# A four-layer sequence model on one core: identity multiplications at the start, diagonals and factors on VectorE, an order table per task

## The chip, the core and the metric

One core of one Trainium2 chip. The metric is the device time of the whole kernel in microseconds; the runs of one kernel in this study spread over 0.2 to 1.3%. Engines in the profile: PE is TensorE, PEld its weight loads, DVE is VectorE, ACT ScalarE, POOL GpSimd, SP the engine that issues most DMAs.

## The reference

Four layers on a sequence of 2048 tokens with 640 features, in bf16: A, B, A, B, each on the normalized input and with a residual.

```python
def _A_ref(x, ...):                      # state space layer ("S5")
    Lam_bar = jnp.exp(dt * Lam)                               # 640 complex numbers
    B_bar = ((Lam_bar - 1.0) / Lam)[:, None] * Bmat           # the "factors" scale B (or C)
    Bu = jnp.einsum("bld,pd->blp", x + 0j, B_bar)
    for t in range(L):
        h = Lam_bar[None, :] * h + Bu[:, t, :]
        ...
    return 2.0 * jnp.einsum("blp,dp->bld", hseq, Cmat).real + x * Dskip[None, None, :]

def _B_ref(q, k, v, ...):                # q, k, v are inputs: the long convolution does not depend on x
    ...                                  # k_shift: shift convolution of k with 4 taps
    kv = k_shift * v
    ...                                  # y: convolution of kv with ssm_k over 2048 steps, by FFT
    y = y + kv * ssm_D[None, None, :]
    return q * y

x = x + _A_ref(_layernorm(x), ...);  x = x + _B_ref(_layernorm(x), ...)
x = x + _A_ref(_layernorm(x), ...);  x = x + _B_ref(_layernorm(x), ...)
```

## The kernel before

The program is a set of tasks with an engine, an estimated duration, dependencies and buffer slots. While it is built, a list scheduler in Python plays them through and so fixes the order of the instructions on each engine; all PSUM is four slots of 128 x 1024 fp32. A table gives each group of tasks a number that makes up most of its rank.

```python
    WHEN = {"yt_io0": -1077.9, ..., "a_lamd": 156.7, "a_f": 165.3, ...}     # subtracted: makes up most of the rank
    ...
    cands = [t for t in ready if eng in t.engs and (t.engs[0] == eng or eng_free[t.engs[0]] > now + 0.3) and can(t)]
    t = max(cands, key=lambda t: (t.rank, -t.idx))
```

The diagonals and factors are made on GpSimd:

```python
    def diag(dst, scal, n):
        nc.gpsimd.tensor_tensor(dst, ident[:, None, :].to_broadcast([P, n, P]), scal[:, :, None].to_broadcast([P, n, P]), ALU.mult)

    def e_lamd(_):                                            # 15 diagonals of 128: "wide diagonals"
        diag(s_ld.get().rearrange("p i j n -> p (i j) n"), st["lam"][:].rearrange("p i j -> p (i j)"), 15)
    t_ld = S.add("a_lamd", "pool", 3.4, [t_lam], e_lamd, uses=[s_ld])

    def e_f(_):                                               # the factors, on 128 x 5 elements
        v = nc.gpsimd
        v.tensor_tensor(den[:], lre, lre, ALU.mult)
        ...                                                   # some 25 more such instructions
    t_f = S.add("a_f", "pool", 5.5, [t_lam], e_f)
    ...
        def e_dk(_, kb=kb, s_ds=s_ds):                        # diagonals of the shift convolution, 512 wide
            nc.gpsimd.tensor_tensor(s_ds.get(), consts["ident_bf"][:, None, :].to_broadcast([P, 4, P]),
                                    st["skf"][:, :, kb:kb + 1].to_broadcast([P, 4, P]), ALU.mult)
```

TensorE multiplies them: the shift convolution is 8 matmuls of 512 columns per half, B times the wide diagonals gives the matrices of the second token phase. A PSUM slot is free for the next group only when ScalarE or VectorE has evicted it. In a B layer each of four rows has its own product and sum on VectorE:

```python
                def e_m(_, q=q, bu=bu):
                    b, x = bu(), s_x.get()[:, q, :]
                    nc.vector.tensor_tensor(b, b, s_Y.get()[:, q, :], ALU.mult)
                    ...                                       # sum with x, by layer
```

Of the kernel before, what the change touches and what calls it, by code (L numbers as in the profile page):

```python
# [17 lines left out]
P = 128  # L18
# [34 lines left out]
    "yt_io0": -1077.9, "yt_ph0": -1019.3, "yt_sin0": 190.5, "yt_neg0": 314.5, "yt_io6": -1435.7, "yt_ph6": -1019.8, "yt_sin6": -1080.4, "yt_neg6": 172.3,  # L53
    "yt_io12": 294.3, "yt_ph12": -1069.6, "yt_sin12": 375.6, "yt_neg12": 156.6, "yt_Ci": 118.7, "yt_Si": 403.1, "yt_nsi": 236.7, "yt_f0": -965, "yt_f2":
    -1540, "yt_f3": -1887, "yt_f4": 179, "yt_h0": 174.5, "yt_h1": 154.3, "yt_h2": 148.5, "yt_h3": 189.9, "kv_dsl": 34.9, "kv_kd": 410.2, "kv_k0": -1067.5,
    "kv_k1": 205.4, "kv_k2": 230.3, "kv_d0": -1030.9, "kv_d1": -1037.8, "kv_d2": 125.1, "kv_ds0": 95.3, "kv_lk0": -919.4, "kv_lv0": 119.4, "kv_mm0":
    -1408, "kv_ev0": 192.8, "kv_st0": -966.5, "kv_ds1": 400.8, "kv_lk1": 143.9, "kv_lv1": 406.3, "kv_mm1": 238.5, "kv_ev1": 232.1, "kv_st1": 180.1,
    "kv_ds2": -1696.5, "kv_lk2": 390.3, "kv_lv2": 173.4, "kv_mm2": 244.3, "kv_ev2": 403.7, "kv_st2": -1020, "kv_ds3": -1063.8, "kv_lk3": -1121.4,
    "kv_lv3": 669.8, "kv_mm3": 420.7, "kv_ev3": -1025, "kv_st3": 1400.2, "kv_ds4": 90.8, "kv_lk4": -926.2, "kv_lv4": 7.3, "kv_mm4": 33, "kv_ev4": -831.9,
    "kv_st4": -980.1, "a_pl": 481.2, "a_p0": -840.7, "a_p1": -1244.2, "a_p2": 1659, "a_p3": 156.5, "a_p4": -793.6, "a_p5": 225.8, "a_p6": -1643.5,  # L60
    "a_lamd": 156.7, "a_f": 165.3, "a_dd": 521.1, "a_ldB0": 150.8, "a_ldB1": -1247.6, "a_wl00": -1403.1, "a_wc00": -1264.8, "a_wm00": 209.8, "a_wl01":
    75.8, "a_wc01": -881, "a_wm01": 418.7, "a_wl02": 307.9, "a_wc02": 301.4, "a_wm02": 403.5, "a_wl03": 164, "a_wc03": -903.2, "a_wm03": -1083.3,
    "a_wl04": 357.2, "a_wc04": -1099.8, "a_wm04": 601.7, "a_b00": 178, "a_b0e0": 230.3, "a_b01": 173.9, "a_b0e1": -1067.1, "a_b10": 69.2, "a_b1e0":
    -1516.7, "a_b11": -1560.6, "a_b1e1": 508.8, "a_gm0": -1359.9, "a_ge0": -1048.3, "a_gm1": -727, "a_ge1": -1525.1, "a_gm2": -1618.5, "a_ge2": -1376.9,
    "a_gm3": -1641.8, "a_ge3": -1386.3, "a_gm4": -1643.2, "a_ge4": -1403, "a_wl10": -2.6, "a_wc10": 155, "a_wm10": -1068.5, "a_wl11": 159.1, "a_wc11":
    -965.4, "a_wm11": 184, "a_wl12": -818.1, "a_wc12": -1242.6, "a_wm12": 79.5, "a_wl13": 104.8, "a_wc13": 414.8, "a_wm13": 181.4, "a_wl14": -1008.6,
    "a_wc14": 26.2, "a_wm14": -1248.1, "a_ti": -1521.4, "a_ta": 395.3, "a_t0": -829.9, "a_t1": 170.8, "a_t2": 613.8, "yq0_kl": -982.4, "yq0_ka": -1602.5,
    "yq0_KA": 159.8, "yq0_KB": 402.8, "yq0_vl": -1113.3, "yq0_VA": 481.3, "yq0_VB": -1118.9, "yq1_kl": 30, "yq1_ka": 311.3, "yq1_KA": -1517.3, "yq1_KB":
    -954.5, "yq0_pw": 209.4, "yq0_IB": 298.2, "yq0_tt": -1552, "yq1_vl": 1519.1, "yq1_VA": -1096.8, "yq1_VB": 420.6, "yq0_IA": 407.6, "yq0_st": -1537.5,
    "yq2_kl": 435.6, "yq2_ka": 157.2, "yq2_KA": 277.9, "yq2_KB": -1166.2, "yq1_pw": 360.8, "yq1_IB": -871.2, "yq1_tt": -1130.5, "yq2_vl": -1467.1,  # L70
    "yq2_VA": 23.2, "yq2_VB": 25.8, "yq1_IA": -1377.8, "yq1_st": -1484.6, "yq3_kl": 498, "yq3_ka": 1686.9, "yq3_KA": 438.7, "yq3_KB": -1402.5, "yq2_pw":
    1355.7, "yq2_IB": -1302.1, "yq2_tt": -1424, "yq3_vl": -834.2, "yq3_VA": 161.1, "yq3_VB": 86.9, "yq2_IA": 2.9, "yq2_st": 300.2, "yq4_kl": -1275,
    "yq4_ka": 618.1, "yq4_KA": -931.8, "yq4_KB": 225.6, "yq3_pw": -1643.5, "yq3_IB": 331.5, "yq3_tt": -814.8, "yq4_vl": -798.8, "yq4_VA": 157.4, "yq4_VB":
    326.4, "yq3_IA": 628.2, "yq3_st": 404.5, "yq4_pw": 594.6, "yq4_IB": 599.4, "yq4_tt": -1071.8, "yq4_IA": 126.1, "yq4_st": -1404, "xl0": -1622.2,
    "A1c0_ln_bn": 302.5, "A1c0_ln_sd": -1096.7, "A1c0_ln_post": -1648.8, "A1c0_id": -1304.5, "A1c0_tu": -1475.7, "A1c0_bp": 10.7, "A1c0_ev": 355.4,
    "A1c0_ri": 62.1, "A1c0_sc": 641.6, "A1c0_cy": 233.1, "A1c0_ro": -1576.9, "A1c0_xr": 396.2, "A1c0_cp": 627.9, "A1c0_xe": -1443.8, "xl1": -978,
    "A1c1_ln_bn": 221, "A1c1_ln_sd": 479.8, "A1c1_ln_post": -942.2, "A1c1_id": 1422.5, "A1c1_tu": -1312.3, "A1c1_bp": 338.4, "A1c1_ev": 192.1, "A1c1_ri":
    1654.8, "A1c1_sc": -1000.3, "A1c1_cy": -1122.1, "A1c1_ro": -1077.3, "A1c1_xr": 627.3, "A1c1_cp": -1539.8, "A1c1_xe": -1077.9, "xl2": -1346.1,
    "A1c2_ln_bn": 611.3, "A1c2_ln_sd": -1123.4, "A1c2_ln_post": 402.2, "A1c2_id": 141, "A1c2_tu": 96.1, "A1c2_bp": 640.8, "A1c2_ev": -867.9, "A1c2_ri":
    22, "A1c2_sc": 40.1, "A1c2_cy": -1431.1, "A1c2_ro": -1012.6, "A1c2_xr": 471.5, "A1c2_cp": -1082.5, "A1c2_xe": -1450.9, "xl3": 672.8, "A1c3_ln_bn":  # L80
    37.8, "A1c3_ln_sd": -1392.7, "A1c3_ln_post": -1339.6, "A1c3_id": 30.4, "A1c3_tu": 252.1, "A1c3_bp": -1329.6, "A1c3_ev": 410.6, "A1c3_ri": -1152.5,
    "A1c3_sc": 383.7, "A1c3_ro": 185.7, "A1c3_xr": 534.8, "A1c3_cp": 257.2, "A1c3_xe": -1166.6, "yl0": 143.2, "B1c0_ln_nm": 627.2, "B1c0_ln_sq": 628.8,
    "B1c0_ln_sd": 604.7, "B1c0_ln_post": 185.1, "B1c0_u": -1662.7, "B1c0_m": 369.5, "A2c0_ln_nm": 202.2, "A2c0_ln_sq": 222, "A2c0_ln_sd": 59.4,
    "A2c0_ln_post": -1459.4, "A2c0_id": 273.5, "A2c0_tu": 215.4, "A2c0_bp": 72.8, "A2c0_ev": -1459.1, "A2c0_ri": -790.3, "A2c0_sc": -1361.1, "A2c0_cy":
    -1371.9, "A2c0_ro": -1371.9, "A2c0_cp": 348.7, "A2c0_xe": 634.5, "yl1": 669.8, "B1c1_ln_nm": 308.3, "B1c1_ln_sq": 369.1, "B1c1_ln_sd": 59.5,
    "B1c1_ln_post": 617.9, "B1c1_u": 409, "B1c1_m": -805.6, "A2c1_ln_nm": -1007.9, "A2c1_ln_sq": 422.1, "A2c1_ln_sd": 197.3, "A2c1_ln_post": 131.4,
    "A2c1_id": 423.7, "A2c1_tu": 550.3, "A2c1_bp": 151.8, "A2c1_ev": 590.1, "A2c1_ri": -1014.6, "A2c1_sc": -1015.2, "A2c1_cy": -1015.5, "A2c1_ro": 641.4,
    "A2c1_cp": 487.2, "A2c1_xe": -1744.8, "yl2": -1648.1, "B1c2_ln_nm": 322.3, "B1c2_ln_sq": -1642.8, "B1c2_ln_sd": -1510.7, "B1c2_ln_post": 363.6,
# [68 lines left out]
class Sched:  # L157
# [3 lines left out]


    DMA = ((1.3, 1.6), (0.8, 1.6))

    base = 0.0

    def __init__(self, tc):
# [1271 lines left out]
```

## Time and profile before

| | kernel before |
|---|---|
| time, median of 4 runs | 360.49 us (360.18 to 360.77) |
| span of the profiled run | 358.5 us |
| matmul work at full clock (from counts and shapes) | 320.6 us |
| first transform group starts | 18.78 us |
| last matmul ends | 347.88 us |

The prediction below shows the main lines. One more view is needed: what TensorE waited for up to 36 us (engine, line, releaser: total us, times, longest).

```profile
PE ps L501 <- POOL b L401: 1.2, 1, 1.2
```

TensorE stood still 1.2 us for GpSimd's wide diagonals (line 401). This is a wait that the change is meant to remove.

**Lateness.** Below I use one number per stage: the start of the stage's first matmul less the work of all matmuls that the program has ahead of it (N / 2.4 + 2.5 ns each, 25 ns at least; multiplications that only keep TensorE busy count as no work). It tells by how much TensorE is late there, whatever caused it. The values before stand in the tables below.

### The profile page before, as it was taken

How to read it: one execution, taken by the hardware profiler on the slowest of the kernel's cores; microseconds unless marked ns; L12 is line 12 of the kernel's file. 1: busy time of each engine (PE TensorE's matmuls, PEld its weight loads, DVE VectorE, ACT ScalarE, POOL GpSimd, SP SyncE). 2: the span in 40 equal slices, each digit the busy share in tenths (PEclk: the TensorE clock that was granted, in tenths of full speed). 3: DMA queues.
4: the chain of work that ended last, by engine and by line, in shares of the span. 5: the costliest groups of instructions: out<-in, count | busy, mean ns of one | idle time of the engine just before them, and what ended most of it. 6: DMA issues, size and time to landing. Idle time of an engine off the chain costs nothing.

```text
span 358.5 us, 8291 instructions
## 1 busy us (share of the span) xinstructions
PE 324.3 (90%) x3467; PEld 242.3 (68%) x3493; DVE 321.8 (90%) x482; ACT 253.2 (71%) x399; POOL 24.4 (7%) x57
## 2 busy tenths in 40 slices
PE   2888899978997989999999999999999999999980
PEld 1357867867685978886776686688655788756550
DVE  8979999777899669989997998999999799999996
ACT  6589976989499999784598199796618681106861
POOL 6447200000000000000000000000000000000000
PEclk9999999999999999999999999999999999999996
DMA  9999999989996970966095722450032043000231
GB/s 202 227 169 190 205 193 196 235 156 201 241 249 125 237 159 2 144 121 206 2 206 140 273 76 48 117 129 2 14 61 76 0 112 112 1 2 0 85 136 73
DMA packets 118711, 45.90 MB, mean 128 GB/s; under 512 B 111629, under 2 KB 112914, under 8 KB 118674
## 3 DMA queue, kind: packets, MB, share of 16 engines
q1 hardware_dynamic: 118528, 45.36, 59.1%
q8 instruction: 27, 0.44, 0.5%
q14 instruction: 10, 0.08, 0.1%
q10 hardware_dynamic: 146, 0.01, 0.0%
HBM read 17.38 MB, written 7.86 MB: 70 GB/s over the span
## 4 chain that ended last, share of the span: by engine, by line
PE 62%; ACT 14%; DVE 11%; DMA 5%; issue 4%; POOL 2%; SPq 1%; ACTq 0%; DVEq 0%; POOLq 0%
PE ps L773 31%; PE ps L687 9%; PE ps L684 9%; ACT b L296 8%; PE ps L522 4%; PE ps L1064 4%; DMA b<-b 2%; DVE b L298 2%; ACT b L466 1%; DMA b<-in_A_C_im_dram 1%; DMA b<-in_A_C_re_dram 1%; SPq L462 1%; PE ps L1214 1%; DVE b L1070 1%; PE ps L1215 1%
## 5 line engine op out<-in xcount | busy, mean ns | idle before, releaser
L296 ACT ACTIVATE b<-ps 128x1024 bf16<-128x1024 f32 (+3 forms) x121 | 105.9, 957 | 28.9 <-PE ps L687 22.2
L773 PEld LDWEIGHTS <-b 128*128 128x128 bf16 x880 | 67.6, 98 | 48.2
L773 PE MATMUL ps<-W,b 128*128 128x512 bf16 (+1 forms) x632 | 95.4, 299 | 0.4
L684 PE MATMUL ps<-b,BT 128*128 128x256 bf16 x400 | 56.7, 273 | 2.4 <-ACT b L296 1.7
L687 PE MATMUL ps<-b,BT 128*128 128x256 bf16 x400 | 56.8, 273 | 0.0
L722 DVE TENSOR_TENSOR_SCAN b<-rtab,b 128x1290 bf16<-128x1290 f32 x16 | 44.6, 2832 | 0.2
L684 PEld LDWEIGHTS <-BT 128*128 128x128 bf16 x400 | 38.7, 98 | 7.2 <-issue 1.8
L687 PEld LDWEIGHTS <-BT 128*128 128x128 bf16 x400 | 39.1, 98 | 4.5
L595 ACT ACTIVATE junk<-b,nmean 128x640 bf16<-128x640 f32 x48 | 39.8, 828 | 1.5
L640 ACT ACTIVATE b<-b,nmr,rstd 128x640 bf16<-128x640 f32 (+1 forms) x42 | 35.7, 916 | 2.8 <-DVE nmr L607 2.0
L1133 PE MATMUL ps<-b,b 128*128 128x128 bf16 x170 | 35.1, 219 | 2.4 <-ACT b L296 1.4
L1136 PE MATMUL ps<-b,b 128*128 128x128 bf16 x170 | 35.3, 219 | 0.0
L1135 PE MATMUL ps<-b,b 128*128 128x128 bf16 x150 | 32.9, 220 | 0.0
L1138 PE MATMUL ps<-b,b 128*128 128x128 bf16 x150 | 32.9, 219 | 0.0
L298 DVE CAST b<-ps 128x1024 bf16<-128x1024 f32 (+2 forms) x28 | 28.0, 1024 | 4.7 <-PE ps L1138 2.3
L781 ACT ACTIVATE b<-ps 128x640 f32<-128x640 f32 x15 | 10.5, 701 | 26.4 <-PE ps L773 26.4
L773 PE MATMUL ps<-G,b 128*128 128x128 bf16 (+1 forms) x151 | 26.5, 295 | 0.5
L1064 PE MATMUL ps<-b,fd 128*128 128x512 bf16 x75 | 20.6, 415 | 2.8 <-ACT b L296 1.9
L470 DVE SCALAR_TENSOR_TENSOR W<-b,s_F 128x640 bf16<-128x640 bf16 x20 | 17.2, 880 | 3.7 <-ACT b L466 3.5
L466 ACT ACTIVATE b<-b,s_F 128x640 f32<-128x640 bf16 x20 | 16.5, 832 | 5.2 <-DMA b<-in_A_C_im_dram 4.0
L590 ACT ACTIVATE nmean<-sums 128x4 f32<-128x4 f32 (+1 forms) x15 | 3.0, 201 | 22.7 <-DVE b L785 19.3
L1214 PE MATMUL ps<-b,b 128*128 128x128 bf16 x160 | 18.4, 220 | 0.5 <-ACT b L296 0.5
(210 smaller groups left out, 571.6 us busy)
## 6 DMA issues: line engine op xcount, KB each, us to landing
b<-in_A_x_dram SPq DMA_DIRECT2D x8, 640.0 KB, 5.9
b<-ysd SPq DMA_DIRECT2D x8, 640.0 KB, 3.9
b<-in_B_ssm_k_dram SPq DMA_DIRECT2D x5, 512.0 KB, 6.4
kvd<-b SPq DMA_DIRECT2D x5, 512.0 KB, 3.8
b<-kvd SPq DMA_DIRECT2D x5, 512.0 KB, 5.1
ysd<-b SPq DMA_DIRECT2D x5, 512.0 KB, 4.6
out_dram<-b SPq DMA_DIRECT2D x8, 320.0 KB, 2.2
W<-in_A_B_im_dram SPq DMA_DIRECT2D x1, 800.0 KB
```

Of the source, the lines that this page charges most:

```text
L296: nc.scalar.activation(out, in_, ACT.Copy)
L298: nc.vector.tensor_copy(out, in_)
L595: nc.scalar.activation(small.junk, src(q), ACT.Square, bias=st["nmean"][:, i:i + 1], scale=1.0, accum_out=st["ssq"][:, i:i + 1])
L640: nc.scalar.activation(dst, src, ACT.Identity, bias=st["nmr"][:, i:i + 1], scale=st["rstd"][:, i:i + 1])
L684: nc.tensor.matmul(pb[:, jj, c2, :], lhsT=aw["BT1"][:, c2, j, k, :], rhs=uT[:, k, 0:2, :].rearrange("p t i -> p (t i)"), start=(k == 0), s ...
L687: nc.tensor.matmul(pb[:, jj, c2, :], lhsT=aw["BT0"][:, c2, k, j * P:(j + 1) * P], rhs=uT[:, k, 2:4, :].rearrange("p t i -> p (t i)"), star ...
L722: nc.vector.tensor_tensor_scan(gv, rt, gv, 0.0, ALU.mult, ALU.add)
L773: nc.tensor.matmul(pc[:, o0:o1], lhsT=lh, rhs=rh, start=(n == 0), stop=(n == len(ops) - 1))
L1064: nc.tensor.matmul(pk[:, 512 * b:512 * (b + 1)], lhsT=s_ds.get()[:, l, :], rhs=kT[:, t0:t0 + 512], start=(l == 0), stop=(l == 3))
L1133: nc.tensor.matmul(ps[:, g, 0, :], lhsT=T["Cf"].get()[:, q, :], rhs=are, start=True, stop=single)
L1135: nc.tensor.matmul(ps[:, g, 0, :], lhsT=T["Sf"].get()[:, q, :], rhs=A[:, 2 * q + 1, :], start=False, stop=True)
L1136: nc.tensor.matmul(ps[:, g, 1, :], lhsT=T["NSf"].get()[:, q, :], rhs=are, start=True, stop=single)
```

## The change

Its intent: TensorE's clock is up when data lands; GpSimd's wide diagonals and factors go to VectorE, which should be faster; the GpSimd diagonals of the convolution are split, so that the first piece comes early; the normalized input is written contiguously; one product of 2560 columns replaces four of 640; and each task gets its own place in the order, planned with better estimates.

```diff
+    s_warm = R_ps.new()
+    def e_warm(_):
+        for i in range(72):
+            nc.tensor.matmul(s_warm.get()[:, P * (i % 4):P * (i % 4 + 1)], lhsT=consts["ident_bf"][:], rhs=consts["ident_bf"][:], start=True, stop=True)
+    S.add("warm", "pe", 2.2, [], e_warm, bias=90000, uses=[s_warm])
...
-        diag(s_ld.get().rearrange("p i j n -> p (i j) n"), st["lam"][:].rearrange("p i j -> p (i j)"), 15)
-    t_ld = S.add("a_lamd", "pool", 3.4, [t_lam], e_lamd, uses=[s_ld])
+        diag(nc.vector, s_ld.get().rearrange("p i j n -> p (i j) n"), st["lam"][:].rearrange("p i j -> p (i j)"), 15)
+    t_ld = S.add("a_lamd", "dve", c_tt(15 * P), [t_lam], e_lamd, uses=[s_ld])
     def e_f(_):
-        v = nc.gpsimd
-    t_f = S.add("a_f", "pool", 5.5, [t_lam], e_f)
+    t_f = S.add("a_f", "dve", 1.9, [t_lam], e_f)
...
-            nc.gpsimd.tensor_tensor(s_ds.get(), consts["ident_bf"][:, None, :].to_broadcast([P, 4, P]),
-                                    st["skf"][:, :, kb:kb + 1].to_broadcast([P, 4, P]), ALU.mult)
+            for l in range(4):
+                nc.gpsimd.tensor_tensor(s_ds.get()[:, l], consts["ident_bf"][:], st["skf"][:, l, kb:kb + 1].to_broadcast([P, P]), ALU.mult)
...
-                ln_apply(nc, eng, st, q, s_u.get()[:, :, slot, :], src(q).rearrange("p (k e) -> p k e", e=P))
+                ln_apply(nc, eng, st, q, s_u.get()[:, slot * D:(slot + 1) * D], src(q))
...
+                def e_mm(_):
+                    b = s_b.get()
+                    nc.vector.tensor_tensor(b, b, s_Y.get(), ALU.mult)
...
-    "yt_io0": -1077.9, "yt_ph0": -1019.3, ...
+    "warm": -5, "yt_io0": 2.55, "yt_ph0": 4.27, ..., "a_b0e0:0": (10.51, 0), ...    (a time per task, and how long it waits for its first engine)
+            t.rank, t.wait = (-when[0], when[1]) if isinstance(when, tuple) else (-when, 0.3)
```

## The prediction

> **What bounds the kernel now.** I read the busy shares first, then the busy times by stretch, then the chain that ended last, then the order of time in the first 30 us and after the last matmul.
>
> The page's first part and three of its slice rows:
>
> ```profile
> PE 324.3 (90%) x3467; PEld 242.3 (68%) x3493; DVE 321.8 (90%) x482; ACT 253.2 (71%) x399; POOL 24.4 (7%) x57
> ...
> PE   2888899978997989999999999999999999999980
> ...
> DVE  8979999777899669989997998999999799999996
> ACT  6589976989499999784598199796618681106861
> ```
>
> Two engines at 90% do not tell which one binds, and a busy PE is not a PE at its peak. Busy time by stretch (the numbers are busy us, with instruction counts, then clock, DMA share, GB/s):
>
> ```profile
> 0.00:20.00 20.00, 10.92 (x70) 5.93 (x71) 17.21 (x51) 12.05 (x16) 11.01 (x25) 1.00 1.01 212
> 20.00:40.00 20.00, 17.16 (x258) 13.63 (x259) 17.43 (x31) 19.37 (x34) 12.25 (x31) 1.00 1.08 194
> 40.00:60.00 20.00, 18.90 (x270) 15.36 (x269) 19.85 (x21) 16.89 (x22) 1.16 (x2) 1.00 1.11 204
> ...
> 100.00:165.00 65.00, 59.38 (x803) 51.89 (x803) 56.57 (x93) 59.77 (x76) 0.00 (x0) 1.00 0.74 157
> ...
> 348.00:358.50 10.50, 0.00 (x0) 0.00 (x0) 7.22 (x14) 1.42 (x4) 0.00 (x0) 0.69 0.24 94
> ```
>
> So I counted PE's work instead: every matmul by shape, times the interval at which a dense stream runs. That interval is in the chain of work that ended last (start us, us, what):
>
> ```profile
> 206.27 0.55 PE ps L684 x5
> ...
> 338.08 3.82 PE ps L773 x28
> 341.92 0.83 DVE b L785 x2
> ```
>
> Five matmuls of 256 columns take 0.55 us, so 0.109 us each; 128 columns then take 0.056 and 512 columns 0.216. Over all 3,492 matmuls of the program that sums to 320.6 us in a span of 358.5. PE therefore waits or runs slowly for only 37.9 us. By stretch (elapsed less work of the matmuls in it; the trace lacks a few, which makes the parts about 1 us too large): 0 to 20 us 13.5; 20 to 100 us 7.5; 100 to 165 us 4.3; 165 to 348 us 3.0; after the last matmul 10.5. From 20 us on PE is already at some 94%, from 165 us at 98%. PE is the bound; a change that does not touch these five gaps cannot move the time.
>
> The start, in order of time (start us, us, engine, line, operation):
>
> ```profile
> 9.86 0.64 POOL L925 TENSOR_SCALAR_AFFINE_SELECT b<-b 128x256 f32<-128x256 f32 x1 [3.00 <-ACT b L919]
> ...
> 12.96 5.89 PE L1064 MATMUL ps<-b,fd 128*128 128x512 bf16 x16 [0.65 <-POOL fd L1041]
> ...
> 28.33 3.39 POOL L401 TENSOR_TENSOR b<-ident_bf,s_lam 128x1920 bf16<-128x1920 bf16 x1 [1.74 <-DVE s_lam L395]
> ...
> 30.42 1.99 DVE L552 TENSOR_SCALAR b<-rtab 128x1290 f32<-128x1290 f32 x1
> ```
>
> The first dense PE work (the shift convolution) begins at 12.96, behind GpSimd, which builds its diagonals only after two selects that wait for a sine. Its 16 matmuls take 5.89 us where 16 x 0.216 = 3.46 is the warm time.
>
> **What the skill says.** (1) "TensorE: Matmul & The Clock Gate", Part 1: the array starts at half clock and needs about 3.4 us of sustained activity to reach full clock; an idle window of that length sends it back. The trace agrees with half clock: the weight loads of those 16 matmuls stand 0.425 us apart up to 17.6 us, twice 0.216. (2) The same page, "Back-to-back issue gap": N/2.4 + 2.5 ns, 109.2 ns at 256 columns; the trace has 0.109 us. (3) "VectorE: DVE Perf Modes", "The perf-mode tier table": a two-tensor bf16 operation runs at two elements a cycle at most, with a fixed start cost. The trace has 487 ns for 640 elements and 1494 ns for 2560, so about 0.15 us fixed and 0.525 ns an element. (4) "GPSIMD Engine Reference", "1. Specifications": GpSimd shares its SBUF interface with VectorE's two-port modes. The trace agrees: the 1290-element fp32 step above took 1.99 us while GpSimd built its diagonals, where the next, a two-input one, took 1.53.
>
> **The change part by part.**
>
> Warm-up: 72 identity matmuls of 128 columns. The bf16 identity is ready at 2.3 us (its cast starts at 1.46 and takes 0.81). If the first 3.4 us run at 0.107 each (32 of them) and 40 at 0.056, it ends near 8 us. PE has no data until 6.4 now, and in the new DMA order the first S5 matrix follows a transposed load, so it lands about 7 to 8: the 4.0 us of added full-clock work costs nothing. It removes 5.89 - 3.46 = 2.4 us, provided that the clock stays up.
>
> The head's order: VectorE now does the small index operations first (15 at about 0.12, then 6 at 0.25, so 3.3 us) ahead of the sine phases. Summing durations of the present trace in the new order: identity 2.3, index work to 5.5, first phase (0.95 + 0.7) to 7.4, cast and angle work (0.5 + 2.25) to 10.1, second phase to 11.8, three small ones to 12.4; only then comes the copy that releases the diagonals on GpSimd (1.3 us). The convolution then starts near 13.9, 0.9 later than now. Its first half ends at 15.6, its second half (behind a copy, an eviction and one S5 group) near 18.3, where the forward transform starts with 5.3 us of real work done; now it starts at 18.78 with 5.0. Net gain of the head: about 0.8 us, not 2.4.
>
> Diagonals (1920 wide): 3.39 us on GpSimd become about 2 on VectorE (the scalar is fp32 and constant along the row, so I count one element a cycle). The exponential also comes earlier. By the same kind of sum they are ready near 29, against 31.7. The 24 factor operations took 31.68 to 38.4 on GpSimd; on VectorE the steps of such small operations are 0.17 to 0.2, so 4.6 us, behind 1.2 of eviction and 2.4 to 3.5 of table work: ready near 37 to 38. They gain little on the path, and cost VectorE 4.6 us in a stretch where it has 37.3 busy of 40 (20 to 60 us). Against that the 1.99 us step should fall towards 0.85.
>
> Layout and merges: the normalised values are written contiguously. On VectorE 5 strided fp32 ones fall from 0.94 to 0.61 and some 6 bf16 ones by about 0.2: 2.8 us. On ScalarE the minimum, median and maximum over both layouts are 904, 908 and 983 ns, so nothing. 28 products of 640 become 7 of 2560: 28 x 0.487 - 7 x 1.494 = 3.2 us off VectorE. Five smaller evictions and one add-reduce move to ScalarE (about 2.6 us). VectorE in all: + 2 + 4.6 - 2.8 - 3.2 - 2.6 = -2.0 us; ScalarE + 2.8. All of it beside a saturated PE after 165 us, so worth almost nothing there.
>
> The order table: the keys of groups become keys of single tasks, so evictions of four PSUM tiles can be interleaved with matmuls as they come free. It acts on the 7.5 + 4.3 = 11.8 us of gaps between 20 and 165 us. Listing both orders, the sequence of PE's work is much the same, with the diagonals' matmuls 3 us of work earlier and the second layer's projection later, so that eviction-heavy and matmul-heavy work alternate more evenly. I take a quarter, 2.8 us, as my choice; no row gives it. Of the 3.0 after 165 us I take 0.3.
>
> The tail. Now VectorE starts the last add-reduce at 348.54 and ends at 355.33 with 7 scalar-tensor operations behind it (0.88 each, started 0.8 apart); the last store ends at 358.5. In the new order all 8 of them stand behind the last add-reduce, and it is preceded by 4.8 us of VectorE work against a last PE group of 4.07. I count 1.0 us lost.
>
> Sum: -0.8 - 2.8 - 0.3 + 1.0 = -2.9 us. With the finer interleaving as likely to be worth more as less, I put 357.2 us, 0.9% under 360.56.
>
> **The rivals.** First, the clock drops again: between 9 and 14 us PE has only 0.6 us of S5 groups, in pieces. I put the longest pause at 2.6 us, under the 3.4 of the skill, but the present trace stays cold through 6.9 to 17 us with PE half busy. If so, the head loses 0.9 + 0.8 instead: about 360. Second, the order removes far more: were the gaps of 20 to 165 us halved and the tail kept, 5.9 + 0.8 off, near 353.5 and about 2%. For it speaks that the estimates in the scheduler are brought near the traced durations; against it, that PE already is at 94%. Third, VectorE becomes the bound between 20 and 60 us through the 6.6 us added there: evictions come late, PE waits for PSUM, up to 3 us lost, near 360.
>
> **Range and chances.** The second rival sets the low end, 352.5; the first and third together the high end, 361.5. Over 2% faster means under 353.35 us, 7.2 of the 37.9 us of gaps, which needs the second rival in full: 0.18. Over 2% slower would need several new waits at once: 0.04.
>
> **What would show it.** The convolution's 16 matmuls: 0.22 us apart (warm) or 0.43 (first rival). Their start near 13.9. The wide diagonals on VectorE, about 2 us, ended near 29. PE's gap by stretch: 12.7 up to 20 us, near 9 for 20 to 165, near 2.7 after. The time from the last matmul to the end: 11 to 12 us. I am wrong if the dense part's gaps change by over 1 us, or if the gaps of 20 to 165 us change by less than 1 or over 5.

## More of the kernel before

One run of the changed kernel took 1197 us and one of the kernel before 688 us, where all others take 354 to 367; such runs count as slow and are in no ratio. Their cause is not known.

## The result and the profile after

358.17 us median (357.78 to 358.61, 4 runs) against 360.49. The ratio is 0.9936, interval 0.9918 to 0.9954; a ratio here is the mean time of one kernel's fast runs over that of the other's of the same rounds, so not quite the ratio of the medians. Same within 2%, and inside the predicted range, 1.0 us above the predicted time.

The page of the changed kernel, busy shares and the clock row (40 slices of the span; 9 is full clock):

```profile
PE 327.5 (92%) x3534; PEld 247.6 (69%) x3565; DVE 315.1 (88%) x479; ACT 256.4 (72%) x406; POOL 20.8 (6%) x51
...
PEclk9999899999999999999999999999999999999996
```

The clock row has an 8 in the fifth slice (35.7 to 44.6 us), which the kernel before does not have. By stretch (us busy, with counts; then clock, DMA share, GB/s):

```profile
20.00:40.00 20.00, 16.34 (x232) 13.21 (x232) 17.01 (x48) 17.84 (x29) 3.46 (x6) 0.92 1.06 210
...
345.00:356.80 11.80, 0.70 (x13) 0.53 (x10) 8.46 (x15) 1.42 (x4) 0.00 (x0) 0.75 0.28 111
```

In 20 to 40 us TensorE has less busy time than before (16.34 against 17.16) at a lower clock (0.92 against 1.00). The start, TensorE in order of time:

```profile
1.78 6.25 PE L1414 MATMUL ps<-ident_bf 128*128 128x128 bf16 x72 [1.78 <-DVE ident_bf L399]
...
14.28 1.61 PE L1163 MATMUL ps<-b,fd 128*128 128x512 bf16 x6 [0.69 <-POOL fd L1141]
...
16.40 1.89 PE L1163 MATMUL ps<-b,fd 128*128 128x512 bf16 x8
18.22 0.65 PE L1208 MATMUL ps<-FA,b 64*128 64x128 bf16 x16
```

The warm-up did its work in this run: the second half of the convolution takes 1.89 us for 8 matmuls, 0.22 apart. The first transform starts at 18.22, 0.56 earlier than before and with 0.3 us more work done. Then VectorE, from the wide diagonals (line 487) to the eviction at line 384; the factors are lines 496 to 525:

```profile
25.48 2.31 DVE L487 TENSOR_TENSOR b<-ident_bf,s_lam 128x1920 bf16<-128x1920 bf16 x1
...
28.85 0.82 DVE L638 TENSOR_SCALAR b<-rtab 128x1290 f32<-128x1290 f32 x1
...
31.12 0.16 DVE L496 TENSOR_TENSOR s_den<-s_pf 128x5 f32<-128x5 f32 x1
...
34.18 0.16 DVE L525 TENSOR_SCALAR s_F<-s_g 128x5 f32<-128x5 f32 x1
34.25 0.72 DVE L991 TENSOR_SCALAR b<-b 128x2176 bf16<-128x2176 bf16 x1
34.88 0.82 DVE L384 CAST BT<-ps 128x640 bf16<-128x640 f32 x1
```

and TensorE behind it:

```profile
27.85 0.23 PE L587 MATMUL ps<-b,tab 128*128 128x128 bf16 x1 [1.26 <-DVE b L487]
...
35.75 0.40 PE L1208 MATMUL ps<-FA,b 64*128 64x128 bf16 x8 [1.69 <-DVE BT L384]
...
37.96 0.31 PE L588 MATMUL ps<-b,W 128*128 128x128 bf16 x1
38.07 0.31 PE L587 MATMUL ps<-b,tab 128*128 128x128 bf16 x1
```

The wait for the wide diagonals is not gone: TensorE stands still 1.26 us for them, now on VectorE, as 1.2 before; but that is at 27.85 us with 12.26 us of work ahead, where it was at 31.77 with 15.22. The factors hold VectorE from 31.12 to 34.34. Behind them waits an eviction; for its PSUM slot TensorE stands still 1.69 us. From 36.9 to 40.3 the matmuls then come 0.107 us apart and not 0.056: the clock fell to half for 3.41 us. The end:

```profile
345.89 0.81 DVE L871 SCALAR_TENSOR_TENSOR b<-ps,b 128x640 f32<-128x640 f32 x1
...
352.72 0.88 DVE L905 SCALAR_TENSOR_TENSOR b<-b,rstd,b 128x640 bf16<-128x640 bf16 x1
```

All 8 scalar-tensor operations stand behind the last add-reduce, as predicted; the last one ends at 353.60, and last matmul to end is 11.1 us against 10.7.

Lateness of TensorE (us) at the seven stages, and the time from the last matmul to the end:

| stage | before | changed |
|---|---|---|
| first transform | 13.80 | 12.93 |
| first product with the wide diagonals | 16.55 | 15.59 |
| first inverse transform | 17.94 | 19.05 |
| first product for G | 21.48 | 21.70 |
| first projection, layer 1 | 22.70 | 22.56 |
| first output product, layer 1 | 27.10 | 24.92 |
| last matmul | 27.27 | 25.09 |
| tail | 10.7 | 11.1 |

The change gains 1.0 us up to the diagonals, loses 2.1 between them and the first inverse transform, gains 3.3 from there to the first output product, and nothing after it. The two values at G can't be compared, since the orders have different numbers of transforms ahead of it, each counted at 0.056 us where it takes about 0.028 us. What went in the stretch with the gain, by TensorE's waits from 54.6 to 164.6 us before and from 54 to 164.1 after (the longest line of each):

```profile
PE ps L1109 <- ACT b L296: 2.4, 4, 0.9
```

```profile
PE ps L1313 <- ACT b L382: 2.1, 1, 2.1
```

TensorE's idle time there fell from 10.0 to 6.9 us. Before, 7.0 of it were 12 waits for evictions on ScalarE, of 0.9 us at most; after, 5.2 are 9 such waits, 2.1 of them in one.

### The profile page after: what moved, and what is told of

It reads as the page before. It is cut to its first block, busy times and chain, and to the rows that moved or that the text cites. A ratio compares the mean times of both kernels' runs of the same rounds, so it can differ in the third digit from the quotient of the medians.

```text
span 356.8 us, 8409 instructions
## 1 busy us (share of the span) xinstructions
PE 327.5 (92%) x3534; PEld 247.6 (69%) x3565; DVE 315.1 (88%) x479; ACT 256.4 (72%) x406; POOL 20.8 (6%) x51
## 4 chain that ended last, share of the span: by engine, by line
PE 69%; ACT 10%; DVE 8%; DMA 7%; issue 3%; SPq 2%; DVEq 0%; ACTq 0%
PE ps L859 31%; PE ps L770 11%; PE ps L773 11%; ACT b L382 6%; PE ps L608 3%; PE ps L1163 3%; DMA b<-in_A_C_im_dram 2%; DMA b<-in_B_v_dram 2%; DVE b L1169 2%; PE ps L1313 2%; DMA b<-b 2%; PE ps L1314 1%; PE ps L1208 1%; SPq L536 1%; DMA b<-in_B_k_dram 1%
## 5 line engine op out<-in xcount | busy, mean ns | idle before, releaser
L382 ACT ACTIVATE b<-ps 128x1024 bf16<-128x1024 f32 (+3 forms) x125 | 109.6, 945 | 29.5 <-PE ps L773 25.5
L859 PE MATMUL ps<-W,b 128*128 128x128 bf16 (+1 forms) x629 | 95.7, 298 | 0.6
L726 ACT ACTIVATE b<-b,nmr,rstd 128x640 bf16<-128x640 f32 (+1 forms) x43 | 37.0, 915 | 6.2 <-DVE nmr L693 6.2
L1232 PE MATMUL ps<-b,b 128*128 128x128 bf16 x170 | 35.1, 219 | 1.2 <-ACT G L382 0.7
L1235 PE MATMUL ps<-b,b 128*128 128x128 bf16 x170 | 35.4, 219 | 0.0
L1237 PE MATMUL ps<-b,b 128*128 128x128 bf16 x150 | 32.8, 219 | 0.0
L1234 PE MATMUL ps<-b,b 128*128 128x128 bf16 x150 | 32.8, 219 | 0.0
L384 DVE CAST b<-ps 128x1024 bf16<-128x1024 f32 (+2 forms) x24 | 26.2, 1109 | 6.3 <-PE ps L1208 2.7
L867 ACT ACTIVATE b<-ps 128x640 f32<-128x640 f32 x16 | 11.1, 697 | 22.8 <-PE ps L859 22.8
L1163 PE MATMUL ps<-b,fd 128*128 128x512 bf16 x73 | 18.6, 380 | 3.8 <-POOL fd L1141 2.0
L1313 PE MATMUL ps<-b,b 128*128 128x128 bf16 x160 | 19.4, 219 | 2.6 <-ACT b L382 2.1
L1314 PE MATMUL ps<-b,b 128*128 128x128 bf16 x160 | 19.2, 219 | 0.0
```

What stands on the lines that cost most here:

```text
L382: nc.scalar.activation(out, in_, ACT.Copy)
L726: nc.scalar.activation(dst, src, ACT.Identity, bias=st["nmr"][:, i:i + 1], scale=st["rstd"][:, i:i + 1])
L859: nc.tensor.matmul(pc[:, o0:o1], lhsT=lh, rhs=rh, start=(n == 0), stop=(n == len(ops) - 1))
L1163: nc.tensor.matmul(pk[:, 512 * b:512 * (b + 1)], lhsT=s_ds.get()[:, l, :], rhs=kT[:, t0:t0 + 512], start=(l == 0), stop=(l == 3))
L1232: nc.tensor.matmul(ps[:, g, 0, :], lhsT=T["Cf"].get()[:, q, :], rhs=are, start=True, stop=single)
L1234: nc.tensor.matmul(ps[:, g, 0, :], lhsT=T["Sf"].get()[:, q, :], rhs=A[:, 2 * q + 1, :], start=False, stop=True)
```

## The experiments

My theory after reading: **T1**, the factors on VectorE cost a wait and a fall of the clock (about 3 us), and the new order pays for it later. Rivals: **T2**, the eviction would have been late anyway; **T3**, the order table is the whole gain and the operations only ride along. All variants of the changed kernel below keep its order on every engine except where the edit says so. Kernels of one call shared a chip and the runs of the kernel before (medians 360.1 to 360.5). The lateness of all profiles stands in one table after the last experiment.

### Without the warm-up

```diff
-        for i in range(72):
+        for i in range(0):
```

> The changed kernel without its 72 warm-up multiplications; every other instruction stays in its place. If the warm-up is worth what the prediction gave it (the clock of the first 16 convolution matmuls), these matmuls stand 0.43 us apart again instead of 0.22, the transform behind them starts 1 to 2 us later than 18.22, and the kernel takes 0.5 to 1.5 us more: 358.7 to 359.7. If the first transform waits for its tables and not for TensorE, the convolution only fills time that is idle anyway and the kernel stays within 0.3 us of 358.2.

Measured: 359.74 us median (358.74 to 359.87), ratio to before 0.998 (0.9956 to 1.0005). TensorE in the profile:

```profile
13.21 3.82 PE L1163 MATMUL ps<-b,fd 128*128 128x512 bf16 x8 [1.19 <-POOL fd L1141]
...
20.00 0.62 PE L1208 MATMUL ps<-FA,b 64*128 64x128 bf16 x16
```

The convolution is cold and the transform starts at 20.00, as the first theory says, 1.78 us later. At the wide diagonals 1.14 us of that are left (lateness 16.73 against 15.59): the changed kernel has waited 0.82 us for ScalarE in between. Then this kernel gets ahead, 18.65 against 19.05 at the first inverse transform, since the changed kernel's profile has its fall of the clock there (1.5 us, below) and this one has its fall at 137.9 us. At the last matmul, with one fall in each, it is 1.32 us behind. The times say the same: about 1.3 us against the changed kernel (ratio 0.9945, below), with intervals that just overlap. That fits the first theory. How much of it is the start's is not shown, since the lateness of the two also changes by 0.95 us between the first inverse transform and G, and I have not traced why.

### Factors on GpSimd again

```diff
     def e_f(_):
+        v = nc.gpsimd
```

> The changed kernel with the factors computed on GpSimd again, in the same place of the order; VectorE loses 29 small instructions (3.2 us from 31.1 to 34.3). Theory 1: the eviction behind them held a PSUM slot, so TensorE's wait of 1.69 us near 34 and the half clock from 36.9 to 40.3 that follows both go; TensorE's gap in 20 to 60 us falls from 6.5 to about 3.7, and the kernel to 355.5 to 357. The table instruction beside GpSimd goes back from 0.82 to about 2.0 us, which takes 1.2 us of VectorE's gain back. Theory 2: another eviction holds the slot as well, the wait stays above 1 us, and the kernel stays at 358.2 within 0.5.

Measured: 357.17 us (356.01 to 360.65), 0.9935 (0.9893 to 0.9977). VectorE, the same eviction:

```profile
33.98 0.82 DVE L384 CAST BT<-ps 128x640 bf16<-128x640 f32 x1 [1.11 <-PE ps L589]
```

It now waits for TensorE, not TensorE for it; no TensorE wait above 0.2 us is left between 29 and 40 us. Lateness between the wide diagonals and the first inverse transform grows by 0.69 us instead of 3.46, and is 22.59 at the last matmul instead of 25.09. T1 holds and T2 falls, for TensorE. The table step (29.79 to 30.61) kept its 0.82 us although the factors on GpSimd ran from 28.96 to 36.1: that part of my expectation was wrong. It was GpSimd that was held up: its operation beside the step took 0.78 us, others of its kind 0.20. The step was slow only beside the wide GpSimd product, 1.99 us before and 3.00 with the order alone, and ended both times 0.69 us after that product. (The trace has 25 small instructions for the factors, not the 29 of the expectation.) The six times spread over 4.6 us and do not by themselves show the gain; in the profiled run the clock fell once, at 15.3 us.

### The same wait, with TensorE kept busy

```diff
-                for o4 in range(4):
+                for o4 in list(range(4)) * (5 if name == "yq0_VA" and g == 0 else 1):
```

> The changed kernel with one group of 8 transform matmuls near 33.7 us done five times over (same result; its PSUM slot is evicted by VectorE at 35.6 anyway), so that TensorE works through most of its wait of 1.69 us. The wait for VectorE stays as it is. If the clock fell because TensorE stood still, it stays at 1.00 from 36.9 to 40.3, the 20 matmuls from 37.24 stand 0.056 us apart and not 0.107, and TensorE is 1.2 to 1.5 us ahead at 43 us; the kernel gains 0.5 to 1.4 us: 356.8 to 357.7. If the clock falls for another reason, or if what comes after waits for ScalarE and VectorE anyway, the time stays at 358.2 within 0.4.

Measured: 357.75 us (356.99 to 358.76), 0.9934 (0.991 to 0.9957). Changed kernel, then this one, from 37 to 41 us:

```profile
37.00:41.00 4.00, 4.00 (x53) 3.48 (x50) 2.14 (x4) 2.80 (x4) 0.00 (x0) 0.59 1.14 176
```

```profile
37.00:41.00 4.00, 3.98 (x78) 3.46 (x78) 3.32 (x5) 3.55 (x4) 0.00 (x0) 1.00 1.28 174
```

78 matmuls against 53 at clock 1.00 against 0.59. TensorE's delay against the changed kernel's profile goes from +1.27 us before the pause to -0.27 after it: the fall had cost 1.5 us. Here the clock fell in the start instead, from 11.9 to 18.7 us, two units of 3.41. The kernel without warm-up has the wait and no fall there, and says the same: from the wide diagonals to the first inverse transform its lateness grows by 1.92 us, as here, and by 3.46 in the changed kernel. So T1's loss has two parts, by the profiles: 1.2 us for the wait (1.92 against 0.69 with the factors on GpSimd) and 1.5 for the fall. The times alone (0.9934 against 0.9945 for the changed kernel, below) do not tell the two kernels apart.

### The order alone

All operations as before, in the order of the changed kernel. Core of the edit:

```diff
-        for i in range(72):
+        for i in range(0):
-        diag(nc.vector, s_ld.get()
+        diag(nc.gpsimd, s_ld.get()
     def e_f(_):
+        v = nc.gpsimd
     ...    (strided layout and 512-wide diagonals as before)
-                    nc.vector.tensor_tensor(b, b, s_Y.get(), ALU.mult)
+                    pass
     ...
+                        nc.vector.tensor_tensor(b, b, s_Y.get()[:, q, :], ALU.mult)
```

> The order of the changed kernel with all operations as before: no warm-up, diagonals and factors on GpSimd, wide diagonals of the convolution in one instruction, strided layout of the normalized input, one product per row. If the order table is the gain (the prediction gave it 2.8 of 2.9 us), this takes 357 to 358.7 and the gap in 60 to 165 us stays near 7.4. If the operations are the gain, it takes 359.5 to 361. A third way: since the factors are off VectorE, the wait near 34 us is gone and it beats the changed kernel: under 357.

Measured: 363.27 us (362.95 to 364.77), 1.0093 (1.0068 to 1.0119): slower than before, outside all three expectations. What TensorE waited for from 20 to 45 us:

```profile
PE ps L587 <- POOL b L487: 2.4, 1, 2.4
PE ps L1208 <- DVE b L1169: 1.4, 2, 1.2
```

The new order puts the products with the wide diagonals 3 us of work earlier (12.26 us of work ahead of them, 15.22 before); with the diagonals on GpSimd they come 2.4 us too late, and the clock falls at 30.8. At the last matmul this kernel is 27.76 late, 0.5 more than before. The other 2.8 us are its tail, 13.5 us against 10.7: there my edit put the four products of a chunk with their sums, behind an add-reduce that they preceded in the plan. The kernel with products in the right place (below) has a tail of 11.4, so about 2.0 us of the 3.1 are my edit's and the order alone is worth about +1.1, which is an estimate. T3 falls either way: the order is no gain without the operations.

### The changed kernel again

> The changed kernel as it is, on the chip of the runs it is to be compared with. Expected 357.5 to 359. If the clock falls where a pause of TensorE happens to fill half of a window of the clock gate, its place differs from that of the first profile (36.9 to 40.3 us): it may be in the head or not there at all, and each such fall lasts 3.41 us or a multiple of it. If the clock falls because of what the kernel does, it is at 36.9 again.

Measured: 358.23 us (357.30 to 358.60 without the run of 1197.28), 0.9945 (0.9927 to 0.9964). The profiled run was the one of 1197 us, so whether the clock falls at 36.9 us again stays unanswered by this run; the profile of the next kernel, which differs little, bears on it.

### Strided layout and four products again

```diff
-                    b = s_b.get()
-                    nc.vector.tensor_tensor(b, b, s_Y.get(), ALU.mult)
+                    for q in range(4):
+                        b = s_b.get()[:, q, :]
+                        nc.vector.tensor_tensor(b, b, s_Y.get()[:, q, :], ALU.mult)
     ...    (strided layout as before)
```

> The changed kernel with the strided layout of the normalized input and with one product per row again (four of 640 where there is one of 2560, in the same place), nothing else. VectorE gets about 6 us of work back. If it lies beside a saturated TensorE, as the prediction says, the time is that of the changed kernel within 0.4 us. If VectorE bounds the end, where 7 us of its work stand behind the last add-reduce, the last product alone brings 4 x 0.487 - 1.494 = 0.45 us and the layout some more: 0.5 to 1.5 us slower, nearly all of it after the last matmul.

Measured: 359.03 us (357.80 to 359.44), 0.9965 (0.9945 to 0.9984), against 0.9945 for the changed kernel in the same rounds. Lateness from the first output product to the last matmul: 25.26 to 25.42, so beside TensorE the 6 us of VectorE work cost nothing, as predicted; the tail grew by 0.3. The difference of the medians (0.8 us) is larger than what the profile accounts for, and the intervals overlap; I take 0.3 as shown. Its clock fell twice, at 14.2 and at 38.05, the second time behind the same pause as in the first profile.

### The operations alone

The kernel before in its own order with the new operations (one product per row stays):

```diff
+            self.warm()                                     # 72 identity multiplications ahead of all tasks
-        nc.gpsimd.tensor_tensor(dst, ident...               # wide diagonals
+        eng.tensor_tensor(dst, ident...                     # eng is VectorE
     def e_f(_):
-        v = nc.gpsimd
     ...    (convolution diagonals in pieces of 128, contiguous layout)
```

> The kernel before in its own order, with the new operations: warm-up first, wide diagonals and factors on VectorE, convolution diagonals in pieces, contiguous layout (one product per row stays, since its order does not allow the merge). If the order table is the gain, this stays within 0.7 us of before: 359.5 to 361. If the operations are the gain, it takes 357.5 to 359. If operations and order only gain together, because the order was tuned with these operations, it is above 360 as the order alone was (363.3).

Measured: 363.89 us (362.47 to 366.93), 1.0124 (1.0088 to 1.0159). TensorE's waits from 20 to 45 us:

```profile
PE ps L502 <- DVE b L299: 2.1, 1, 2.1
PE ps L1110 <- DVE b L299: 1.2, 1, 1.2
```

Both are VectorE evictions behind diagonals and factors. At the first transform this kernel is 0.5 us ahead of before (13.28 late); from the first product with the wide diagonals to the first inverse transform its lateness grows by 4.14 us against 1.39. The clock fell at 12.5, 32.9 and 118.3 us. So the order alone loses, the operations alone lose 3.7 us, and together they gain 2: neither has a price of its own.

### A first attempt at a version that beats both

```diff
     def e_f(_):
+        v = nc.gpsimd
-        for i in range(72):
+        for i in range(88):
+                if kb == 0 and h == 0:
+                    fill(nc, consts["ident_bf"][:], pk, 20)       # 20 identity multiplications ahead of the convolution
+                if c == 0 and j == 2:
+                    fill(nc, ident[:], s_pb.get(), 20)            # and ahead of the products with the wide diagonals
+        nc.vector.tensor_tensor(st["ds0"].get(), ...)             # first convolution diagonals, right behind their copy
-                    nc.vector.scalar_tensor_tensor(bu(), s_x..., st["nmean"]..., s_Y..., ALU.add, ALU.mult)
+                    ln_apply(nc, "act", st, i, bu(), s_x.get()[:, q, :])      # last chunk: normalize on ScalarE,
+                    nc.vector.tensor_tensor(...)                              # product and sum on VectorE
```

> The changed kernel with four changes that the runs suggest: the factors on GpSimd; identity multiplications also in the pauses before the convolution and before the wide diagonals, and 88 instead of 72 at the start, against a fall of the clock; the first convolution's diagonals in one instruction on VectorE right behind the copy that they wait for, not on GpSimd; and in the last chunk the normalisation on ScalarE, so that VectorE has 5.6 us behind the last add-reduce and not 7.0. Expected by parts: 1.9 for the factors, 1.5 for the clock, 1 to 2 for the earlier convolution, 1.4 for the end, so 352.3 to 354.5. If the head waits for its tables and B's second half whatever the convolution does, 354.5 to 356.

Measured: 357.41 us (356.02 to 360.62), 0.9936 (0.9901 to 0.9972): no better than the changed kernel, a miss. The convolution did start earlier (12.36) and the transform at 17.52, but then TensorE waited 1.68 us for ScalarE, which was at a table load of 1.28 us; the clock fell at 20.5 and again at 136.6. The tail shrank by only 0.5 us, because VectorE waited 0.99 us for the last normalization.

### Fillers alone

The changed kernel with those identity multiplications, and with two transform groups done five times over.

```diff
+                rep = {("yq0_VA", 0): 5, ("yq0_KA", 0): 5}.get((name, g), 1)
-                for o4 in range(4):
+                for o4 in list(range(4)) * rep:
     ...    (88 multiplications at the start and 2 x 20 later, as above)
```

> The changed kernel with TensorE kept busy in its long pauses up to 36 us, with nothing else moved: 88 identity multiplications at the start instead of 72, 20 in front of the convolution, 20 in front of the wide diagonals, and two transform groups, whose eviction comes late anyway, done five times over. The same waits remain. If the falls of the clock (3.41 us at half speed, at a different place in each profile) come from pauses that fill about half of a window of the clock gate, no fall is left before 130 us, and the kernel gains 1 to 2 us over the changed one on this chip (358.2): 356.2 to 357.2, with less spread. If the falls do not depend on such pauses, or if the extra work delays what follows, 358 to 359.

Measured: 360.36 us (358.83 to 360.74), 0.9992 (0.9963 to 1.002): slower than the changed kernel, a miss for both theories. The profile (a run of 359.09) has no fall before 130 us, as the first theory says, and TensorE is 18.02 late at the first inverse transform against 19.05. Then this wait comes:

```profile
PE ps L1323 <- ACT b L387: 2.0, 1, 2.0
```

It is in the changed kernel too (2.1 us near 135), but here the clock fell behind it (136.3 to 139.7), and at the first output product the kernel is 25.48 late against 24.92. Four of the six runs took another 1.1 to 1.7 us. Three of these have a mean granted clock of 0.977 or 0.978, the profiled run 0.987. That is about 16 us at half clock (the time before the first rise is not counted), more than the whole tail and one fall together (14.5), so each had at least one fall more. Whether that is all of the difference is open.

### Factors on VectorE, but in its idle time

```diff
-    t_f = S.add("a_f", "dve", 1.9, [t_lam], e_f)
+    S.f_parts = {"a_b1e0:3": e_f0, "yq1_ka": e_f1, "yq1_VB:e4": e_f2}        # emitted behind these tasks
+    t_f = S.add("a_f", "dve", 1.9, [t_lam], lambda _: None)
```

> The changed kernel with the factors still on VectorE, but in three parts where the order leaves VectorE idle: behind the eviction that TensorE waited for near 34 us, behind the small addition after the next one, and near 62 us for the part that is needed after 110 us. If the place of the 3.2 us and not the engine was the fault, TensorE's wait of 1.69 us is under 0.5 us and the kernel is about as fast as with the factors on GpSimd: 356.3 to 357.5. If VectorE has no slack there, another eviction comes late by as much: 358 within 0.5.

Measured: 357.66 us (356.91 to 359.37), 0.9928 (0.9899 to 0.9957). The wait of 1.69 us is gone (the longest that TensorE waits there for an eviction on VectorE is 0.7), and lateness at the first inverse transform is 17.40, as good as with GpSimd (17.22). So it was the place of the 3.2 us and not the engine. The clock fell at 135.6 us; the end is 24.43 late. The time is 0.2 us above the range that I had given, and does not stand apart from the changed kernel's.

### The version that beats both

To the first attempt: one transform group ahead of the table load five times over, the square root and its statistics behind the evictions that TensorE waits for, and the last statistics earlier.

```diff
+        for nm, after in (("A1c2_ln_sd", "yq3_IB:e3"), ("A1c2_ln_post", "yq3_IB:e4")):
+            ...                                              # move the task behind the other in the order
-    "B2c32_ln_post": 347.34
+    "B2c32_ln_post": 343.5
+                rep = {("yq0_KA", 0): 5}.get((name, g), 1)
```

> A version meant to beat both. As the first attempt (factors on GpSimd, identity multiplications in pauses, the first convolution's diagonals on VectorE, last normalisations on ScalarE), with what its profile showed mended: the transform group ahead of ScalarE's table load is done five times over, so that the pause of 1.7 us near 19 us does not stop the clock; a square root with its table load of 1.28 us goes behind the evictions that TensorE waits for (2.0 us near 133 to 137); and the last statistics are read earlier, so that VectorE does not wait 0.99 us at the end. Against the first attempt's profile (two falls of the clock, 1.5 each; 1.5 for the pause near 135; 0.7 at the end) it should take 352 to 354.5. If the falls remain, 355 to 357.

Measured: 354.77 us (354.70 to 355.58, 5 runs), 0.9847 (0.9822 to 0.9872): about 1.0% under the changed kernel (0.9945) and 1.5% under the one before, and 0.3 us above the range expected without falls. The edits were made together, so their shares are not shown. The clock row and VectorE's end:

```profile
PEclk9999999999999999999999999999999999999996
```

```profile
344.53 0.82 DVE L883 SCALAR_TENSOR_TENSOR b<-ps,b 128x640 f32<-128x640 f32 x1
...
349.85 0.82 DVE L918 TENSOR_TENSOR b<-b,b 128x640 bf16<-128x640 bf16 x1
```

No fall of the clock in this run, and the last VectorE operation ends 6.1 us after the start of the last add-reduce, against 7.7. The tail is 9.5 us against 11.1. The wait near 133 us is only down to 1.7. Two other runs (354.70 and 354.77 us) have a mean clock of 0.985, some 10.6 us at half clock where the tail is 9.5 long, so they probably had a fall and were no slower: that the absent fall makes this version fast is not shown.

### The same without any multiplication for the clock

```diff
-        for i in range(88):
+        for i in range(0):
     ...    (no fillers, no repeated group)
```

> The version that beats both (354.77 us, 0.9847 of before) without any multiplication that only keeps TensorE busy: no warm-up, none in the pauses, no group repeated. The rest and the order stay. If the clock at the start is worth something by itself, the first convolution's matmuls stand 0.43 us apart, the first transform starts 1.5 to 2 us later than 17.6, the second convolution 0.5 to 1 us later than 21.75, and the kernel takes 355.3 to 356.5. If ScalarE and the transfers set the start anyway, so that a cold first convolution fits into time that is idle otherwise, it stays within 0.3 us of 354.8.

Measured: 355.51 us (354.54 to 356.50), 0.9874 (0.9851 to 0.9898). TensorE:

```profile
12.37 2.33 PE L1176 MATMUL ps<-b,fd 128*128 128x512 bf16 x8
15.65 1.89 PE L1176 MATMUL ps<-b,fd 128*128 128x512 bf16 x8
```

The clock came up within the first half of the convolution without any warm-up, and no fall followed; the last matmul is 23.30 late, with warm-up and fillers 23.73. The intervals of the two overlap. The time lies in the range of the first theory, the profile (transform at 17.48 us, second convolution at 21.54) is that of the second. The identity multiplications are not shown to be worth anything in this version.

### All profiles

Lateness of TensorE in us, the tail, and where the clock fell for 3.41 us (twice that where two are joined). Each row is one profiled run; other runs of the same kernel can have other falls.

| kernel | first transform | wide diagonals | first inverse | G | projection | output | last matmul | tail | clock falls at |
|---|---|---|---|---|---|---|---|---|---|
| before | 13.80 | 16.55 | 17.94 | 21.48 | 22.70 | 27.10 | 27.27 | 10.7 | none |
| changed | 12.93 | 15.59 | 19.05 | 21.70 | 22.56 | 24.92 | 25.09 | 11.1 | 36.9 |
| no warm-up | 14.71 | 16.73 | 18.65 | 22.25 | 22.78 | 26.25 | 26.41 | 11.1 | 137.9 |
| factors on GpSimd | 14.51 | 16.53 | 17.22 | 19.87 | 20.40 | 22.42 | 22.59 | 11.1 | 15.3 |
| kept busy | 14.85 | 16.86 | 18.78 | 21.43 | 21.97 | 24.28 | 24.44 | 11.1 | 11.9 (twice) |
| order alone | 14.46 | 18.12 | 20.42 | 23.71 | 25.63 | 27.60 | 27.76 | 13.5 | 30.8 |
| layout, products | 14.28 | 16.30 | 19.75 | 22.39 | 23.24 | 25.26 | 25.42 | 11.4 | 14.2, 38.05 |
| operations alone | 13.28 | 16.88 | 21.02 | 23.46 | 25.28 | 29.32 | 29.49 | 10.7 | 12.5, 32.9, 118.3 |
| first attempt | 12.23 | 16.82 | 17.50 | 21.17 | 22.01 | 25.51 | 25.68 | 10.6 | 20.5, 136.6 |
| fillers alone | 12.95 | 16.52 | 18.02 | 20.66 | 21.19 | 25.48 | 25.65 | 11.1 | 136.3 |
| factors in idle time | 12.95 | 16.22 | 17.40 | 20.27 | 20.81 | 24.26 | 24.43 | 11.1 | 135.6 |
| best | 12.33 | 16.24 | 16.92 | 20.37 | 21.21 | 23.56 | 23.73 | 9.5 | none |
| best, cold | 12.19 | 15.62 | 16.30 | 20.43 | 20.97 | 23.13 | 23.30 | 9.5 | none |

## Why the prediction was right, and which of its steps were not

The sum of the profile is -1.74 us of span against the predicted -2.9; the times gave -2.3. My terms sum to 357.7 us; the 357.2 that I put has 0.5 us more that no term carries. Step by step:

- **TensorE is the bound: right after 165 us**, and more so than I wrote. The 3.0 us of gaps there do not exist: lateness grows by 0.17 us from the first output product to the last matmul in both kernels. The trace lacks 26 of the program's 3,493 matmuls (I had counted 3,492), and I took missing records for gaps. The term of -0.3 was 0. **Before 165 us I made the bound too tight:** the sum of 320.6 us takes 0.056 us for each of the 320 transform matmuls, which start in pairs every 0.056. Estimated with 0.028 it is 311.7 us, TensorE's gaps are 46.8 us and not 37.9, and between 20 and 165 us they are about 22 us and not 11.8: there TensorE worked some 85% of the time, not 94%.
- **Head, -0.8: right in size at its mark** (-0.87 at the first transform). The convolution started at 13.20 and not 13.9, the transform at 18.22 as predicted (18.3), warm, 0.22 us apart. By stretch, though, the gap up to 20 us hardly changed (13.7 before, 13.5 after, the warm-up's 4.0 us of work not counted), where I had put 12.7: after 18.2 us TensorE waits 0.82 us for ScalarE. And the warm clock is luck of the run: with the same 72 multiplications it fell again before the transform in three other profiles (factors on GpSimd, kept busy, layout), and the first transform was 1.3 to 1.9 us later.
- **Wide diagonals, about 2 us, ready near 29: close.** 2.31 us, ready at 27.8; the step of 1.99 us on the table fell to 0.82, as predicted (0.85).
- **Factors, 4.6 us, ready 37 to 38, "gain little on the path": this step failed.** They took 3.2 us and were ready at 34.3, so they are cheaper than I said, but they stand ahead of an eviction: 1.69 us of wait, and a fall of the clock worth 1.5. I had that as the third rival (VectorE late with evictions between 20 and 60 us) and left it out of the sum. Against the kernel before, 2.1 us are lost between the diagonals and the first inverse transform. The new plan has an estimate of 1.9 us for them and expects that eviction at 30.8 us; in the trace it came at 34.9. Of these 4.1 us about 1.2 are the factors', 1.1 the wide diagonals', planned at 1.1 us and traced at 2.3, and the rest was there when the diagonals started.
- **Order table, -2.8, "a quarter, as my choice": this step failed as a term of a sum.** From the first inverse transform to the first output product the changed kernel gains 3.3 us; with the 2.1 lost ahead of it, that is -1.2; counted from 20 to 165 us, as I had forecast it, about -2.0, within the 1 to 5 that I had named. The experiments show that the term cannot be split off: the order with the old operations does not gain (about +1.1 by my estimate, +3.1 as run), the new operations in the old order lose 3.7, both together gain 2.
- **Layout and merges, "worth almost nothing there": right** (0 beside TensorE, 0.3 in the tail), though VectorE's busy time fell by 6.7 us and not by 2.0.
- **Tail, +1.0: too large.** All 8 operations do stand behind the last add-reduce; it cost 0.4.
- **First rival, the clock: right in kind, wrong in its rule.** I let pauses under 3.4 us pass as harmless (the longest in the head was 1.28, where I had put 2.6), from the Trainium skill, "TensorE: Matmul & The Clock Gate", Part 1, which says that the array slows down after at least one idle window of some 3.4 us and that the window is free-running. The runs agree on the second point: each fall lasts 3.413 us or twice that, and its place changes from run to run. On the first they do not: the falls at 36.9 and 38.05 followed a single pause of 1.69 us.

The number came out right because the steps that failed had opposite signs: a loss that I had among the rivals, and a larger gain behind it than the quarter I chose. That they nearly cancel is luck.

What stays open: when exactly a pause stops the clock. The traces narrow it. In each profile the clock changes on a grid of 3.413 us, whose place differs from run to run. All 14 falls follow a grid step in which TensorE was idle for 1.61 us or more. Near 133 us a pause of 2.0 us, or little more, stands in eight profiles. In the four with a fall (no warm-up, first attempt, fillers alone, factors in idle time) it lies whole in one step; in the four without (changed, factors on GpSimd, kept busy, layout) the grid cuts it, and no step has more than 1.88 us. So in these eight the same pause stops the clock or not by where the grid falls, and one kernel's profile without a fall proves little: the kernel without warm-up has the wait of 1.69 us for that eviction too, cut by the grid (1.37 in one step), and no fall there. But idle time in a step is not the whole rule, since 1.61 to 1.76 us were enough for a fall before 40 us and up to 1.88 were not later on.

## What to carry to other kernels

Work that moves to a faster engine is paid for by whatever stands behind it in that engine's queue: look for the eviction or copy next in line and who waits for it, and give the planner the traced duration of a chain of tiny instructions (3.2 us here, not 1.9). Parts of a change that were tuned together have no separate prices; test each alone before adding terms. And find lateness by stage from the work ahead of it, not gaps from busy time: it sees past missing records, and it shows where a gain is given back. Take the time per matmul of each shape from the trace: pairs that run side by side cost half.

## What the Trainium skill lacked or had wrong

- "TensorE: Matmul & The Clock Gate" (Part 1, the table of the two states) gives at least one idle window of about 3.4 us as the condition for half clock. Here a pause of 1.69 us was enough (falls at 36.9 and 38.05 us), and one of 2.02 us elsewhere, cut by the grid, was not. A later section of the page has a clock that goes up and down with frequent short pauses, but no figure for how much idle time in a window is enough. The length of a fall, 3.413 us or a multiple, agrees with the page's window.
- The same page warns that the first rise to full clock varies from run to run. No page that I read warns that later falls do too, so that variants of one kernel cannot be compared by time alone: a single fall cost 1.5 us here where it was measured, 0.4% of the time, and falls lay anywhere between 11.9 and 137.9 us in the profiles.
- "GPSIMD Engine Reference" (3.1) puts elementwise work with two inputs at about half VectorE's speed. Its figure is for fp32; here the wide diagonals in bf16 took 3.39 us on GpSimd and 2.31 on VectorE, a factor of 1.5 (2.15 without GpSimd beside it, in the operations alone). Operations on 128 x 5 elements took 0.20 against 0.16 to 0.17 us each, but the chain of factors 6.7 us on GpSimd before and 3.2 on VectorE. That the two share an SBUF interface (its part 1) agrees: of four GpSimd products of 128 columns beside VectorE's wide diagonals one took 2.31 us, as long as the VectorE instruction, the others 0.39.
- "GPSIMD Engine Reference" (3.1) names a cost for each instruction on GpSimd without a figure, so what splitting a wide product costs can't be read from it: four of 128 columns took 4 x 0.39 = 1.6 us, one of 512 took 1.05.
